# Softmax by pairs of tiles, the V halo sent ahead of the LN2 transposes, and h added to b2 by an accumulating DMA

## The chip, the cores and the metric

The kernel runs on one core of one Trainium2 chip. The metric is the time of one execution on the device, in microseconds (us). A profile comes from one of these executions. Its span is about 1.8 us shorter than the time that the device reports, so spans are compared with spans and times with times. Unless said otherwise, every execution named here was fast: within 1.5% of the fastest run of its kernel.

TensorE is called PE below, VectorE DVE, ScalarE ACT. SP is the engine that issues most DMAs, and POOL is GpSimd. The kernel has PE's sums written into PSUM, in pairs of banks named A to D, and uses a pair again once another engine has read it.

## The reference

One transformer layer on x of shape (1, 2048, 576), in bf16:

```python
h  = x + attention(layernorm(x)) @ wo      # 32 heads of 18, each position sees itself and 7 earlier ones, 2 apart
h2 = h + gelu(layernorm(h) @ w1 + b1) @ w2 + b2     # 4608 hidden units
```

The softmax of a position runs over 8 logits for each head.

## The kernel before

The 2048 positions are 16 tiles of 128, worked off as eight groups of two tiles. For each group PE does three things in a row: the first MLP matmul (L209, output `pm`), the output projection of the tiles of the *next* group (`pw`), and the second MLP matmul (`po`). The attention of the group after the next, and the second layernorm (LN2) of the next group, are meant to hide under these on DVE, ACT, POOL and the DMA engines.

This is how one group's normalized input `hnT` comes about, and PE's next group starts with it (shortened; `rstd` is one over the standard deviation of a row):

```python
def ln2_act(j):                 # statistics on ACT, rstd on POOL
    nc.scalar.activation(out=y, in_=h, func=Identity, scale=-1/D, accum_out=nmean)
    nc.scalar.activation(out=y, in_=h, func=Square, bias=nmean, accum_out=var)
    nc.scalar.activation(out=var, in_=var, func=Identity, scale=(1+EPS)/D, bias=eps2)
    nc.gpsimd.tensor_tensor(out=rstd, in0=var, in1=mhalf, op=ALU.pow)

def ln2_send(j):                # normalized rows to DRAM
    nc.scalar.activation(out=nmean, in_=nmean, func=Identity, scale=rstd)
    ln_apply_act(y, h, rstd, nmean)
    hn[j] = dma_out(y)          # two stores into td

def ln2_in(j):                  # and back, transposed
    nc.sync.dma_start_transpose(out=hnT_slot(j), in_=hn.pop(j))

def add_b2(j):                  # x of a tile becomes h + b2, the residual of the output
    nc.vector.tensor_tensor(out=x_all[:, j, :], in0=h_of.pop(j), in1=b2_bc, op=ALU.add)
```

The keys and values of 8 tiles lie in a ring. When tile j is done with the keys (or values), a DMA, the halo, replaces its slot by the same rows shifted by one, which the following tile of the same parity needs:

```python
def halo(j, t):                 # t = 1: keys, t = 2: values
    if j >= 2:
        ring = (None, k_ring, v_ring)[t]
        nc.sync.dma_start(out=ring[j % 2][:, j // 2, :], in_=kv_dram[j, 0:P, t - 1, :])
```

With c, d the tiles of the next group and e, f those of the one after, a middle group runs as follows (paraphrased; a visit is one of the parts into which the first matmul is cut; `m1[v]`: before visit v; `ia`, `ib`: before matmul row n of the second one, for its first and second tile):

```python
m1[0]: finish_out(previous), pv_t(d)                 # sums over V of the group's second tile
m1[3]: att_qk(e), w2_sums
ia[0]: exps(e), wo_visit(c, d), ln2_pair(c, d), att_den(e)
ia[2]: pv_sum(e), dma_tr_o(e)
ib[0]: finish_out(first)                             # output add: frees PSUM pair D
ib[2]: att_qk(f)
ib[32]: exps(f)
```

Of the kernel before, what the change touches and what calls it, by code (L numbers as in the profile page):

```python
# [17 lines left out]
def kernel(  # L18
# [13 lines left out]
    P = 128  # L32
# [49 lines left out]
    prod = wpool.tile([P, W, D], BF16, name="prod")  # L82

# [55 lines left out]
    def ln_stats(srcs, tag, c1, c0, bufs, first=None):  # L139
        n = len(srcs)  # L140
        stats = sb.tile([P, n, 2, nc.vector.BN_STATS_DIM], F32, tag=f"{tag}_stats", name=f"{tag}_stats", bufs=bufs)
        mv = sb.tile([P, n, nc.vector.BN_AGGR_DIM], F32, tag=f"{tag}_mv", name=f"{tag}_mv", bufs=bufs)
# [39 lines left out]

    def dma_out(src):
        td = dram.tile([P, KT * P], BF16, tag="td", name="td", bufs=4)
        nc.sync.dma_start(out=td[:, 0:D], in_=src)
        nc.sync.dma_start(out=td[:, D:KT * P], in_=src[:, KF * P:D])
        return td
# [121 lines left out]
    e_of = {}  # L309
# [16 lines left out]
    def att_qk_b(j, skip=0):  # L326
        att_qk_add(j, ((0, 0, 9), (0, 0, 4), (0, 0, 2), (0, 0, 1))[skip:])
        logits = sb.tile([P, W, H], F32, tag="logits", name="logits", bufs=2)
        nc.vector.tensor_tensor(out=logits[:], in0=prod[:, :, 0:H], in1=prod[:, :, 8 * H:9 * H], op=ALU.add)
        if j // 2 + 1 < W:  # L330
            nc.vector.memset(logits[0:1, j // 2 + 1:W, :], -1e9)
        mx = sb.tile([P, H], F32, tag="mx", name="mx")
        nc.vector.tensor_reduce(out=mx[:], in_=logits[:].rearrange("p w h -> p h w"), axis=AX.X, op=ALU.max)
        nc.vector.tensor_tensor(out=logits[:], in0=logits[:], in1=mx[:].unsqueeze(1).to_broadcast([P, W, H]),  # L334
                                op=ALU.subtract)
        e_of[j] = logits

    def att_qk(j):
        att_qk_a(j)
        halo(j, 1)  # L340
        att_qk_b(j)

    def att_exp(j):
        logits = e_of[j]
        nc.scalar.activation(out=logits[:], in_=logits[:], func=ACT.Exp, scale=SCALE)  # L345
# [5 lines left out]
    def att_den(j):  # L351
        e = e_of.pop(j)
        den = sb.tile([P, H], F32, tag="den", name="den")
        nc.vector.tensor_reduce(out=den[:], in_=e[:].rearrange("p w h -> p h w"), axis=AX.X, op=ALU.add)
        nc.vector.reciprocal(out=den[:], in_=den[:])
        a = sb.tile([P, W, H], BF16, tag="a", name="a")
        nc.vector.tensor_tensor(out=a[:], in0=e[:], in1=den[:].unsqueeze(1).to_broadcast([P, W, H]), op=ALU.mult)
        e_of[j] = a

    def att_pv_sum(j):  # L360
        a = e_of.pop(j)
        nc.vector.tensor_tensor(out=prod[:].rearrange("p w (d h) -> p w d h", h=H),  # L362
                                in0=v_ring[j % 2].rearrange("p w (d h) -> p w d h", h=H),
                                in1=a[:].unsqueeze(2).to_broadcast([P, W, Dh, H]), op=ALU.mult)
# [70 lines left out]
    def add_b2(j):  # L435
        nc.vector.tensor_tensor(out=x_all[:, j, :], in0=h_of.pop(j)[:], in1=b2_bc[:], op=ALU.add)

# [202 lines left out]
    with tc.manual_schedule(engines={ENG.PE, ENG.Activation, ENG.DVE, ENG.SP, ENG.Pool}):  # L640
# [83 lines left out]
        def ln2_pair(c, d, e, b2=True):  # L724
# [3 lines left out]
            for j in (c, d):  # L728
                if b2:
                    add_b2(j)  # L730
                ln2_send(j)
            for j in (c, d):
                ln2_in(j)
            if e is not None:
                att_den(e)

        loads = {v: [c_(load_w1, c)] for c, v in enumerate((3, 4, 9, 14, 16, 18))}
        for n, v in enumerate((20, 21, 22, 23)):
# [9 lines left out]
            7: [c_(att_qk_b, A[0]), c_(ln1_bias, 10), c_(ln1_act, 8, 3), c_(in_x, 0), c_(out_x, 1)],  # L748
            8: [c_(att_qk_a, A[1]), c_(att_qk_b, A[1]), c_(ln1_act, 9, 0)],
# [11 lines left out]
            20: [c_(ln2_rstd, A[1]), c_(add_b2, A[1]), c_(ln2_bias, A[1]), c_(att_qk_b, A[2], 1)],  # L761
# [57 lines left out]
        def exps(j):  # L819
            att_exp(j)  # L820
            gelu_table()
# [7 lines left out]
        for k, g in enumerate(GROUPS):  # L829
# [6 lines left out]
            if k == 0:  # L836
                m1[0] += [c_(halos, 1), c_(att_qk_a, d), c_(att_qk_b, d), c_(halo, d, 1)]
# [61 lines left out]
```

## Time and profile before

Time: 371.6 us (371.4 to 372.2, four runs), span 369.8 us.

From the page of the kernel before, the busy time of each engine with its share of the span and its number of instructions, and the shares of the chain of work that ended last:

```profile
PE 363.2 (98%) x4944; PEld 299.4 (81%) x4944; DVE 299.3 (81%) x452; ACT 239.1 (65%) x519; POOL 25.2 (7%) x35
...
PE 84%; DVE 11%; ACT 2%; POOL 1%; issue 1%; POOLq 0%; DVEq 0%
```

From the waits of PE in the kernel before (who waited for whom: us in total, times, longest):

```profile
PE busy L661 <- DVE prod L654: 1.5, 1, 1.5
PE pm L209 <- ACT hT L490: 0.5, 1, 0.5
PE o_pt L176 <- DVE h L407: 0.3, 1, 0.3
...
```

From its chain in order of time (start, length, what), one whole period of 37.7 us:

```profile
221.95 17.79 PE pm L209 x324
239.74 2.21 PE pw L209 x36
241.95 17.75 PE po L505 x144
259.70 17.79 PE pm L209 x324
```

PE is 98% busy, and from 79 to 366 us the chain is PE matmul but for a few pieces of 0.04 us or less. PE waits for nobody there. Whatever the other engines save cannot shorten this kernel; what they do too late can lengthen it. The slack is how long before PE starts on a group its `hnT` has landed.

PE's timeline, where it starts on it:

```profile
297.37 0.61 PE L209 MATMUL pm<-hnT,w_sb 64*128 64x256 bf16 x8
```

The second transpose is issued at 291.8 and lands 2.8 us later, at 294.6. PE starts at 297.4. The slack is 2.8 us. It is not the same in each group: worked out the same way it is 0.2 us for the second group, 2.8 for the fourth, 1.9 for the fifth, 2.4 for the sixth, and 0.8 for the eighth. For the third, the trace has lost a landing.

### The profile page before, as it was taken

What the parts mean: (1) busy time and instruction counts of PE and PEld (TensorE: products, weight loads), DVE (VectorE), ACT (ScalarE), POOL (GpSimd) and SP (SyncE); (2) the same over time, 40 slices, a digit from 0 to 9 for tenths busy, and PEclk for the clock granted to TensorE, in tenths of its full rate; (3) what the DMA queues carried; (4) which work ended last, traced back from release to release, by engine and by line L of the source; (5) the groups of instructions that cost most, each with busy time, mean ns of one, the idle gap of its engine ahead of it and who ended that gap; (6) DMA issues with size and microseconds to landing.
All of it is one profiled execution on the core that took longest, in us unless ns stands there. A gap on an engine that the chain in (4) does not pass through costs nothing.

```text
span 369.8 us, 11478 instructions
## 1 busy us (share of the span) xinstructions
PE 363.2 (98%) x4944; PEld 299.4 (81%) x4944; DVE 299.3 (81%) x452; ACT 239.1 (65%) x519; POOL 25.2 (7%) x35
## 2 busy tenths in 40 slices
PE   7999999999999999999999999999999999999996
PEld 4789877888788877887788778877887788778874
DVE  6899999999999798979897989889898986532332
ACT  2688756797738793679366936693669456735630
POOL 2322004000300010001000100000000000000000
PEclk9999999999999999999999999999999999999999
DMA  8979798956445104710431043104320411030000
GB/s 242 318 198 282 190 204 235 331 178 76 141 107 166 35 15 111 275 35 2 110 97 37 2 106 102 37 2 105 86 52 3 105 52 39 0 89 18 4 0 32
DMA packets 57265, 38.96 MB, mean 105 GB/s; under 512 B 31344, under 2 KB 55536, under 8 KB 57216
## 3 DMA queue, kind: packets, MB, share of 16 engines
q1 hardware_dynamic: 57056, 38.18, 38.6%
q8 instruction: 38, 0.62, 0.7%
q10 hardware_dynamic: 160, 0.07, 0.1%
q14 instruction: 11, 0.09, 0.1%
HBM read 19.92 MB, written 12.42 MB: 87 GB/s over the span
## 4 chain that ended last, share of the span: by engine, by line
PE 84%; DVE 11%; ACT 2%; POOL 1%; issue 1%; POOLq 0%; DVEq 0%
PE pm L209 37%; PE po L505 29%; PE po L576 8%; PE pw L209 5%; PE pq L209 4%; DVE ln_stats L145 2%; DVE prod L323 2%; DVE prod L362 1%; DVE prod L317 1%; PE busy L661 1%; DVE prod L366 1%; POOL ln_rstd L156 1%; ACT hT L490 1%; DVE ln_mv L146 1%; ACT L463 0%
## 5 line engine op out<-in xcount | busy, mean ns | idle before, releaser
L209 PE MATMUL pm<-hnT,w_sb 64*128 64x256 bf16 x2304 | 143.0, 269 | 0.5 <-ACT hT L490 0.5
L490 ACT ACTIVATE hT<-pm,b_sb 128x256 bf16<-128x256 f32 (+1 forms) x288 | 108.5, 498 | 48.4 <-PE pm L209 48.4
L209 PEld LDWEIGHTS <-w_sb 64*128 64x128 bf16 x2304 | 112.5, 94 | 15.0 <-issue 2.3
L505 PEld LDWEIGHTS <-hT 128*128 128x128 bf16 x864 | 84.0, 98 | 22.6 <-issue 1.7
L505 PE MATMUL po<-w2a_sb,hT 128*128 128x288 bf16 x672 | 84.5, 286 | 0.0
L209 PE MATMUL pq<-wq_sb,xnT 64*128 64x288 bf16 x768 | 54.0, 283 | 0.4 <-ACT xnT L255 0.2
L209 PEld LDWEIGHTS <-xnT 64*128 64x128 bf16 x864 | 44.1, 94 | 9.1 <-issue 0.4
L323 DVE TENSOR_TENSOR prod<-prod 128x2304 bf16<-128x2304 bf16 (+1 forms) x64 | 44.2, 691 | 2.1
L362 DVE TENSOR_TENSOR prod<-kv_ring,a 128x4608 bf16<-128x4608 bf16 x16 | 40.9, 2558 | 0.6
L317 DVE TENSOR_TENSOR prod<-kv_ring,q_all 128x4608 bf16<-128x4608 bf16 x16 | 40.8, 2552 | 0.2
L209 PE MATMUL pm<-hnT,w1h_sb 64*128 64x256 bf16 x288 | 39.4, 269 | 0.0
L366 DVE TENSOR_TENSOR prod<-prod 128x2304 bf16<-128x2304 bf16 (+1 forms) x32 | 33.9, 1058 | 1.1
L345 ACT ACTIVATE logits<-logits 128x256 f32<-128x256 f32 x16 | 6.7, 417 | 38.1 <-DVE logits L334 38.1
L423 POOL TENSOR_TENSOR ln_rstd<-ln_var,mhalf 128x1 f32<-128x1 f32 x14 | 11.3, 810 | 249.8 <-ACT ln_var L422 249.6
L505 PE MATMUL po<-w2b_sb,hT 128*128 128x288 bf16 x192 | 25.5, 286 | 0.0
L294 ACT CAST kv_ring<-pq 128x576 bf16<-128x576 f32 x32 | 19.4, 641 | 8.4 <-PE pq L209 8.4
L407 DVE TENSOR_TENSOR h<-pw,x_all 128x576 f32<-128x576 f32 x16 | 11.4, 751 | 14.0 <-PE pw L209 14.0
L209 PE MATMUL pw<-wo_sb,oT 64*128 64x288 bf16 x256 | 19.5, 283 | 0.2
L463 ACT ACT_TABLE_LOAD x14 | 18.0, 1283 | 0.2
L552 DVE TENSOR_TENSOR prod<-hT 128x512 f16<-128x512 f16 (+1 forms) x8 | 3.6, 455 | 17.6 <-ACT hT L490 17.6
L209 PEld LDWEIGHTS <-oT 64*128 64x128 bf16 x288 | 13.9, 94 | 4.3 <-POOLq L219 0.8
L345 ACT ACT_TABLE_LOAD x13 | 16.7, 1283 | 0.2
(98 smaller groups left out, 340.4 us busy)
## 6 DMA issues: line engine op xcount, KB each, us to landing
w_sb<-in_B_w_dram SPq DMA_DIRECT2D x6, 768.0 KB, 6.0
kv_ring<-kv_dram SPq DMA_DIRECT2D x28, 144.0 KB, 2.8
w2a_sb<-in_B_w_dram SPq DMA_DIRECT2D x4, 1008.0 KB, 6.5
kv_dram<-kv_ring SPq DMA_DIRECT2D x13, 288.0 KB, 3.5
out_dram<-o_sb SPq DMA_DIRECT2D x15, 144.0 KB, 2.9
td<-q_all SPq DMA_DIRECT2D x14, 144.0 KB, 2.4
td<-hn SPq DMA_DIRECT2D x14, 144.0 KB, 1.8
wq_sb<-in_A_wqkv_dram SPq DMA_DIRECT2D x3, 576.0 KB, 5.9
```

The costliest lines, as they stand in the source:

```text
L209: last = nc.tensor.matmul(duo["g"][r ^ swap][i], lhsT=lhsT, rhs=rhs, start=(swap == 0 and i == 0 and kt == 0), stop=(swap == 1 and kt == K ...
L294: pace[0] = nc.scalar.copy(out=dst.rearrange("p (d g h) -> p g d h", g=2, h=H // 2), in_=ps[:, :, 0:HALF].rearrange("p g (h d) -> p g d h" ...
L317: nc.vector.tensor_tensor(out=prod[:], in0=k_ring[j % 2], in1=q_all[:, j, :].unsqueeze(1) .to_broadcast([P, W, D]), op=ALU.mult)
L323: nc.vector.tensor_tensor(out=prod[:, :, o * H:o * H + n], in0=prod[:, :, a * H:a * H + n], in1=prod[:, :, c * H:c * H + n], op=ALU.add)
L345: nc.scalar.activation(out=logits[:], in_=logits[:], func=ACT.Exp, scale=SCALE)
L362: nc.vector.tensor_tensor(out=prod[:].rearrange("p w (d h) -> p w d h", h=H), in0=v_ring[j % 2].rearrange("p w (d h) -> p w d h", h=H), in ...
L366: nc.vector.tensor_tensor(out=prod[:, 0:n, :], in0=prod[:, 0:n, :], in1=prod[:, n:2 * n, :], op=ALU.add)
L407: nc.vector.tensor_tensor(out=h[:].rearrange("p (g c) -> p g c", g=2), in0=pw[:, :, 0:HALF], in1=x_all[:, j, :].rearrange("p (g c) -> p g ...
L463: nc.scalar.activation(out=warm[:], in_=mhalf[:], func=ACT.Gelu_apprx_tanh)
L490: pace[0] = nc.scalar.activation(out=hT[us[i // GF]][:, GF * r + i % GF, 0:N], in_=ps[:, r, i * N:(i + 1) * N], func=ACT.Gelu_apprx_tanh, ...
L505: nc.tensor.matmul(banks[half], lhsT=hT[f // (2 * GF)][:, f % (2 * GF), i * P:(i + 1) * P], rhs=w2_rows(f)[:, half * HALF:(half + 1) * HAL ...
L576: nc.tensor.matmul(bank, lhsT=l, rhs=r, start=(start and m == 0), stop=(m == NM - 1), skip_group_check=True)
```

## The change

The intent is to relieve DVE and ACT. From the second group on the two tiles e, f of a pair share one maximum, exponential, denominator and division (on 512 columns instead of twice 256). The 14 late additions of b2 leave DVE: SP copies b2 into x, and an accumulating DMA from GpSimd adds h, after the stores of LN2. The V halo of e is issued ahead of the LN2 transposes, so that f's sum over V, which now follows soon after e's, finds it. The core of the diff, with cuts:

```diff
+    def put_b2(j):
+        nc.sync.dma_start(out=x_all[:, j, :], in_=b2_bc[:])
+
+    def accumulate_h(j):
+        ins = nc.gpsimd.dma_start(out=x_all[:, j, :], in_=h_of.pop(j)[:], accum_op=ALU.add).ins
+        tc.add_manual_dep(ins, sent[0].name, sync_dep, reason="behind the transfers of LN2")
 ...
-        def ln2_pair(c, d, e, b2=True):
+        def ln2_pair(c, d, js=()):
             for j in (c, d):
                 ln2_h(j)
                 ln2_act(j)
             for j in (c, d):
-                if b2:
-                    add_b2(j)
+                put_b2(j)
+            if js:
+                att_den(*js)
+                att_pv_sum(js[0])
+            for j in (c, d):
                 ln2_send(j)
             for j in (c, d):
+                accumulate_h(j)
+            if js:
+                halo(js[0], 2)
+            for j in (c, d):
                 ln2_in(j)
-            if e is not None:
-                att_den(e)
+            if js:
+                dma_tr_o(js[0])
 ...
-                    m1[3] = m1.get(3, []) + [c_(att_qk, e)] + [c_(w2_sums, *m) for m in T_SUMS.get(k, ())]
-                    ia[0] = [c_(exps, e)]
-                ia[0] = ia.get(0, []) + [c_(wo_visit, (c, "B"), (d, "C")), c_(ln2_pair, c, d, e)]
 ...
+                elif e is not None:
+                    m1[1] = [c_(att_qk_pair, e, f)]
+                    m1[3] = [c_(w2_sums, *m) for m in T_SUMS.get(k, ())]
+                    ia[0] = [c_(exps, e, f), wo, c_(ln2_pair, c, d, (e, f))]
 ...
-                    ia[2] = [c_(pv_sum, e), c_(dma_tr_o, e)]
-                    ib[2] = [c_(att_qk, f)] + ([c_(halos, 7)] if k == 1 else [])
-                    ib[32] = [c_(exps, f)]
+                    ib[2] = [c_(pv_sum, f), c_(dma_tr_o, f)]
```

`att_qk_pair(e, f)` does the key products of e, issues e's K halo, finishes e's logits, and goes straight on to f, which needs that halo. The second group has an order of its own: there the exponential of the pair comes after LN2.

More of the change, by code (lines that the diff above doesn't have):

```diff
@@ L82 @@
     prod = wpool.tile([P, W, D], BF16, name="prod")
+    logits = wpool.tile([P, 2, W, H], F32, name="logits")
+    probs = wpool.tile([P, 2, W, H], BF16, name="probs")
+    peak = wpool.tile([P, 2, H], F32, name="peak")
+    den = wpool.tile([P, 2, H], F32, name="den")
     qp_cm = tc.tile_pool(name="qkvw", bufs=1)
@@ L140, in ln_stats @@
         n = len(srcs)
-        stats = sb.tile([P, n, 2, nc.vector.BN_STATS_DIM], F32, tag=f"{tag}_stats", name=f"{tag}_stats", bufs=bufs)
-        mv = sb.tile([P, n, nc.vector.BN_AGGR_DIM], F32, tag=f"{tag}_mv", name=f"{tag}_mv", bufs=bufs)
+        pool = qp if tag.startswith("ln1") else sb
+        stats = pool.tile([P, n, 2, nc.vector.BN_STATS_DIM], F32, tag=f"{tag}_stats", name=f"{tag}_stats", bufs=bufs)
+        mv = pool.tile([P, n, nc.vector.BN_AGGR_DIM], F32, tag=f"{tag}_mv", name=f"{tag}_mv", bufs=bufs)
         for i, src in enumerate(srcs):
@@ L180, in transpose_in @@
         nc.tensor.transpose(pt[0:HP, KF, :], src[:, KF * P:D], ident[:])
+    sent = [None]
     def dma_out(src):
@@ L185, in dma_out @@
         nc.sync.dma_start(out=td[:, 0:D], in_=src)
-        nc.sync.dma_start(out=td[:, D:KT * P], in_=src[:, KF * P:D])
+        sent[0] = nc.sync.dma_start(out=td[:, D:KT * P], in_=src[:, KF * P:D]).ins
         return td
@@ L306, in tr_b1, with sides @@
         nc.scalar.copy(out=b1_sb[:], in_=pt)
-    e_of = {}
+    side = {}
+    def sides(js):
+        i = side[js[0]]
+        return slice(i, i + len(js))
     def halo(j, t):
@@ L324, in att_qk_add, with att_qk_b, att_max, att_qk_rest @@
                                     in1=prod[:, :, c * H:c * H + n], op=ALU.add)
-    def att_qk_b(j, skip=0):
+    def att_qk_b(j, i, skip=0):
+        side[j] = i
         att_qk_add(j, ((0, 0, 9), (0, 0, 4), (0, 0, 2), (0, 0, 1))[skip:])
-        logits = sb.tile([P, W, H], F32, tag="logits", name="logits", bufs=2)
-        nc.vector.tensor_tensor(out=logits[:], in0=prod[:, :, 0:H], in1=prod[:, :, 8 * H:9 * H], op=ALU.add)
+        nc.vector.tensor_tensor(out=logits[:, i], in0=prod[:, :, 0:H], in1=prod[:, :, 8 * H:9 * H], op=ALU.add)
         if j // 2 + 1 < W:
-            nc.vector.memset(logits[0:1, j // 2 + 1:W, :], -1e9)
-        mx = sb.tile([P, H], F32, tag="mx", name="mx")
-        nc.vector.tensor_reduce(out=mx[:], in_=logits[:].rearrange("p w h -> p h w"), axis=AX.X, op=ALU.max)
-        nc.vector.tensor_tensor(out=logits[:], in0=logits[:], in1=mx[:].unsqueeze(1).to_broadcast([P, W, H]),
-                                op=ALU.subtract)
-        e_of[j] = logits
-    def att_qk(j):
+            nc.vector.memset(logits[0:1, i, j // 2 + 1:W, :], -1e9)
+    def att_max(js):
+        n, sl = len(js), sides(js)
+        nc.vector.tensor_reduce(out=peak[:, sl], in_=logits[:, sl].rearrange("p i w h -> p i h w"), axis=AX.X, op=ALU.max)
+        nc.vector.tensor_tensor(out=logits[:, sl], in0=logits[:, sl],
+                                in1=peak[:, sl].unsqueeze(2).to_broadcast([P, n, W, H]), op=ALU.subtract)
+    def att_qk_rest(j, i, skip=0):
+        att_qk_b(j, i, skip)
+        att_max([j])
+    def att_qk(j, i):
         att_qk_a(j)
         halo(j, 1)
-        att_qk_b(j)
-    def att_exp(j):
-        logits = e_of[j]
-        nc.scalar.activation(out=logits[:], in_=logits[:], func=ACT.Exp, scale=SCALE)
+        att_qk_rest(j, i)
+    def att_qk_pair(e, f):
+        for i, j in enumerate((e, f)):
+            att_qk_a(j)
+            halo(j, 1)
+            att_qk_b(j, i)
+        att_max([e, f])
+    def att_exp(*js):
+        sl = sides(js)
+        nc.scalar.activation(out=logits[:, sl], in_=logits[:, sl], func=ACT.Exp, scale=SCALE)
     def att_pv(j):
@@ L349, in att_pv, with att_den @@
         att_pv_sum(j)
-    def att_den(j):
-        e = e_of.pop(j)
-        den = sb.tile([P, H], F32, tag="den", name="den")
-        nc.vector.tensor_reduce(out=den[:], in_=e[:].rearrange("p w h -> p h w"), axis=AX.X, op=ALU.add)
-        nc.vector.reciprocal(out=den[:], in_=den[:])
-        a = sb.tile([P, W, H], BF16, tag="a", name="a")
-        nc.vector.tensor_tensor(out=a[:], in0=e[:], in1=den[:].unsqueeze(1).to_broadcast([P, W, H]), op=ALU.mult)
-        e_of[j] = a
+    def att_den(*js):
+        n, sl = len(js), sides(js)
+        nc.vector.tensor_reduce(out=den[:, sl], in_=logits[:, sl].rearrange("p i w h -> p i h w"), axis=AX.X, op=ALU.add)
+        nc.vector.reciprocal(out=den[:, sl], in_=den[:, sl])
+        nc.vector.tensor_tensor(out=probs[:, sl], in0=logits[:, sl],
+                                in1=den[:, sl].unsqueeze(2).to_broadcast([P, n, W, H]), op=ALU.mult)
     def att_pv_sum(j):
-        a = e_of.pop(j)
+        a = probs[:, side.pop(j)]
         nc.vector.tensor_tensor(out=prod[:].rearrange("p w (d h) -> p w d h", h=H),
                                 in0=v_ring[j % 2].rearrange("p w (d h) -> p w d h", h=H),
-                                in1=a[:].unsqueeze(2).to_broadcast([P, W, Dh, H]), op=ALU.mult)
+                                in1=a.unsqueeze(2).to_broadcast([P, W, Dh, H]), op=ALU.mult)
         for n in (4, 2):
@@ L747 @@
             6: [c_(ln1_rstd, 10), c_(ln1_act, 8, 2), c_(halo, A[0], 1)],
-            7: [c_(att_qk_b, A[0]), c_(ln1_bias, 10), c_(ln1_act, 8, 3), c_(in_x, 0), c_(out_x, 1)],
-            8: [c_(att_qk_a, A[1]), c_(att_qk_b, A[1]), c_(ln1_act, 9, 0)],
+            7: [c_(att_qk_rest, A[0], 0), c_(ln1_bias, 10), c_(ln1_act, 8, 3), c_(in_x, 0), c_(out_x, 1)],
+            8: [c_(att_qk_a, A[1]), c_(att_qk_rest, A[1], 1), c_(ln1_act, 9, 0)],
             9: [c_(halo, A[1], 1), c_(in_x, 1)],
@@ L760 @@
             19: [c_(ln2, A[1])],
-            20: [c_(ln2_rstd, A[1]), c_(add_b2, A[1]), c_(ln2_bias, A[1]), c_(att_qk_b, A[2], 1)],
+            20: [c_(ln2_rstd, A[1]), c_(add_b2, A[1]), c_(ln2_bias, A[1]), c_(att_qk_rest, A[2], 0, 1)],
         }
@@ L817, in halos, with exps @@
                 store_halo(pending_halo.pop(0))
-        def exps(j):
-            att_exp(j)
+        def exps(*js):
+            att_exp(*js)
             gelu_table()
@@ L836 @@
             if k == 0:
-                m1[0] += [c_(halos, 1), c_(att_qk_a, d), c_(att_qk_b, d), c_(halo, d, 1)]
+                m1[0] += [c_(halos, 1), c_(att_qk_a, d), c_(att_qk_rest, d, 1), c_(halo, d, 1)]
                 mid[0] = [c_(exps, d)]
-                m1[1] = [c_(pv_t, c), c_(pv_t, d), c_(load_w2, 4), c_(att_qk, e)]
+                m1[1] = [c_(pv_t, c), c_(pv_t, d), c_(load_w2, 4), c_(att_qk, e, 0)]
                 ia[0] = [c_(wo_visit, (c, "B"))]
-                ia[12] = [c_(exps, e), c_(wo_visit, (d, "A")), c_(ln2_pair, c, d, e, False), c_(pv_sum, e), c_(dma_tr_o, e), c_(halos, 2)]
+                ia[12] = [c_(exps, e), c_(wo_visit, (d, "A")), c_(ln2_pair, c, d, (e,)), c_(halos, 2)]
@@ L842 @@
                 ib[0] = [c_(finish_out, g[0])]
-                ib[4] = [c_(att_qk, f)]
+                ib[4] = [c_(att_qk, f, 1)]
                 ib[32] = [c_(exps, f)]
             elif c is not None:
-                m1[0].append(c_(pv_t, d))
+                wo = c_(wo_visit, (c, "B"), (d, "C"))
                 if k == 1:
-                    m1[0] += [c_(add_b2, j) for j in g]
-                if e is not None:
-                    m1[3] = m1.get(3, []) + [c_(att_qk, e)] + [c_(w2_sums, *m) for m in T_SUMS.get(k, ())]
-                    ia[0] = [c_(exps, e)]
@@ L852 @@
-                ia[0] = ia.get(0, []) + [c_(wo_visit, (c, "B"), (d, "C")), c_(ln2_pair, c, d, e)]
+                    m1[0].append(c_(pv_t, d))
+                    m1[1] = [c_(att_qk_a, e), c_(halo, e, 1), c_(att_qk_b, e, 0), c_(halos, 7)]
+                    m1[3] = [c_(att_qk_a, f), c_(halo, f, 1)]
+                    ia[0] = [wo, c_(ln2_pair, c, d), c_(att_qk_b, f, 1), c_(att_max, (e, f)), c_(exps, e, f), c_(att_den, e, f)]
+                    ia[2] = [c_(pv_sum, e), c_(dma_tr_o, e)]
+                elif e is not None:
+                    m1[1] = [c_(att_qk_pair, e, f)]
+                    m1[3] = [c_(w2_sums, *m) for m in T_SUMS.get(k, ())]
+                    ia[0] = [c_(exps, e, f), wo, c_(ln2_pair, c, d, (e, f))]
+                else:
+                    ia[0] = [wo, c_(ln2_pair, c, d)]
```

## The prediction

> **What bounds the kernel.** TensorE. The page gives PE 98% busy. In the chain of waits everything from 79 to 366 us is PE matmul without a gap. PE's waits for other engines add to 2.7 us, 1.5 us of it before the first matmul; none is listed after 73 us. A period of one group is 37.7 us (17.8 first MLP matmul, 2.2 output projection, 17.7 second), run five times, then two shorter ones. DVE (81%) and ACT (65%) matter only where they make PE wait.
>
> **What the change removes.** The 14 late b2 adds: 0.75 us each, 10.5 us of DVE. In the five pairs from the second group on, ten softmaxes become five: from the 256- and 576-column f32 operations (425 and 751 ns) an operation costs about 0.16 us beside its columns, so five merged operations save about 0.8 us a pair, 4 us in all. On ACT one exponential with its two table loads and the dummy GELU (1.28+1.28+0.20+0.16 us) goes per pair: about 14 us. Expect DVE busy near 285 us, ACT near 225 us.
>
> **What it adds.** Per group two SP copies of b2 into x, and two accumulating DMAs from GpSimd. The Trainium skill ("DMA: Bandwidth & Descriptors", "SWDGE vs HWDGE vs iDMA") says that accumulation and casting must be issued from GpSimd, and that all issuers share the same 16 DMA engines; the trace of before has no such DMA, so their length is unknown. They wait for the LN2 stores, so they run while the LN2 transposes do.
>
> **What lies on the critical path.** Nothing of the savings: PE has no wait that they could end. The deadlines are what count:
> 1. LN2 transposes. In the timeline of the fourth group they are issued by SP at 215.7 and 217.0 us and land 2.9 us later, about 220.0; PE starts on them at 221.9. Slack 1.9 us. For the last group it is about 0.8 us (issued 328.0 and 329.3, needed at 333.0). The doubled exponential delays ACT by about 0.27 us, the V halo costs SP 0.5 us that it spends waiting anyway, and the accumulates compete for DMA engines: I guess 0.3 to 1 us. So the slack is mostly eaten; a PE wait of 0 to 0.5 us is possible, likeliest in the last group.
> 2. In the second group the pair is late on DVE: exponential near 137 us, sums over V end near 150.5, so the output add that frees PSUM pair C ends near 151.3; PE wants C near 151.5. Wait 0 to 0.5 us.
> 3. Later groups: the second sum over V waits for the halo (lands about 3 us after 215.2), ends near 223; the add that frees C ends near 224, wanted at 227. Fits.
> 4. GpSimd carries the markers between matmul halves. Both accumulates should be issued by 219, the next marker is due at 223. Fits.
>
> **Predicted time.** 371.8 us, range 370.0 to 374.5. Faster by over 2%: 0.01; within 2%: 0.92; slower by over 2%: 0.07.
>
> **What would show each step.** PE still 98%, chain still bare matmul, DVE down about 14 us and ACT about 14 us: right. A PE wait for the DMA of hnT at the start of a group's first MLP matmul: point 1 was too kind. PE waiting for the output add at the start of the third group: point 2. PE waiting for GpSimd's queue: point 4. Start-up to 108 us should be unchanged within 0.5 us.
>
> **What would make it wrong.** Accumulating DMAs that take 4 us or more each and hold up the transposes: 1 to 2 us a group, 7 to 14 us in all. Or GpSimd held up while generating descriptors.

## More of the kernel before

`h` is a tile with two buffers. The last two groups use a faster scheme for the second matmul, whose two remainder buffers `rest` and `part` share the buffers of `h`:

```python
rest, part = (sb.tile([P, D], F32, tag="h", name="rest", bufs=2) for _ in range(2))
```

The start of the seventh group (group 6, counted from 0) serves as the example. First, SP's timeline of the kernel before (start, length on the queue, instruction, output<-input): two stores for each tile, the second tile's at 289.50, and then both transposes.

```profile
289.50 0.33 SPq L185 DMA_DIRECT2D td<-hn  x1
289.89 0.42 SPq L186 DMA_DIRECT2D td<-hn  x1
290.48 2.52 SPq L433 DMA_TRANSPOSE hnT<-td  x2
293.10 0.53 SPq L314 DMA_DIRECT2D kv_ring<-kv_dram  x1
```

The instructions on tile hnT in that window (duration, first and last start; then the time from issue to landing):

```profile
L433 SPq DMA_TRANSPOSE hnT<-td x2: 1204/1216/1227, 290.5 to 291.8; - x2
...
DMA to landing us min/median/max: 2.8/2.8/2.8
```

## The result, and the profile after

The changed kernel takes 376.2 us (374.3, 376.7, 375.7, 377.5) against 371.6 us. The ratio of the fast runs is 1.012 (95% interval 1.009 to 1.015). Here and below a ratio is the mean time of one kernel's fast runs over that of the other's in the same rounds, so it is not quite the ratio of the medians quoted. The change is 1.2% slower: within the 2% band, but outside the range predicted (370.0 to 374.5). It also scatters over 3 us where the kernel before keeps within 0.8.

The profile of the changed kernel fell on the fastest of these runs (374.27 us, span 372.5). From its page, the busy times, the chain, and the two large DMA queues (packets, MB, share of 16 engines' span):

```profile
PE 362.7 (97%) x4944; PEld 303.0 (81%) x4944; DVE 285.8 (77%) x413; ACT 225.0 (60%) x499; POOL 43.2 (12%) x49
...
q1 hardware_dynamic: 59072, 40.24, 40.3%
q0 software_dynamic: 2016, 2.07, 5.1%
...
PE 55%; DVE 28%; DMA 5%; ACT 4%; issue 3%; POOL 2%; SPq 2%; POOLq 0%; DVEq 0%; ACTq 0%
```

The savings came in full: DVE 299.3 to 285.8 us, ACT 239.1 to 225.0. But the chain is no longer bare matmul; 45% of it is now something else (16% before, nearly all of that ahead of 79 us), most of it DVE. The waits of PE in that profile:

```profile
PE pm L216 <- DVE rest L627: 1.2, 1, 1.2
...
PE pm L216 <- DVE logits L342: 0.6, 1, 0.6
...
PE pm L216 <- DMA hnT<-td: 0.3, 1, 0.3
```

(L216 is the line of the matmul that was L209.) The wait put down to `logits L342` is at the start of the second group, where the last transpose landed at 109.12 us, 0.14 us before PE began. Nothing in that matmul reads `logits`, so this too is a wait for `hnT`, put down to something that happened to end at the time.

**Second look, the same kernel.**

> The changed kernel unedited, for its spread and a second trace. Expected as in the first four runs: median near 376 us, runs from 374 to 378, while the kernel before keeps within 0.3 us of 371.6. Both theories expect the PE waits at the start of a group's first MLP matmul (hnT arriving late) and at the start of the last group; a slower execution should show more or longer ones of these.

It took 376.3 us (376.0 to 376.7, four runs), ratio 1.012 (1.011 to 1.013). Its profile (span 374.4 us) has the waits of PE:

```profile
PE pm L216 <- DMA hnT<-td: 2.6, 3, 1.3
PE busy L689 <- DVE prod L682: 1.5, 1, 1.5
PE pm L216 <- DVE rest L627: 1.0, 1, 1.0
```

By group the waits at the start of the first MLP matmul are 1.3 us (second group), 0.35 (fourth), 0.9 (seventh), and 1.0 for the remainder buffers (eighth), together 3.6 of the 4.6 us by which the span grew. Another 0.5 us had arisen before the second group, in the loading phase, which differs by up to 0.9 us between the traces and has nothing to do with the change; the rest is spread in pieces below 0.35 us.

The same group as before, the seventh, in this second profile. SP's timeline:

```profile
293.68 0.33 SPq L192 DMA_DIRECT2D td<-hn  x1
294.06 0.43 SPq L193 DMA_DIRECT2D td<-hn  x1
294.59 0.40 SPq L325 DMA_DIRECT2D kv_ring<-kv_dram  x1
295.16 2.54 SPq L454 DMA_TRANSPOSE hnT<-td  x2
```

The instructions on tile hnT in this window:

```profile
L454 SPq DMA_TRANSPOSE hnT<-td x2: 1212/1217/1222, 295.2 to 296.5; - x2
...
DMA to landing us min/median/max: 2.8/3.5/4.1
```

PE's timeline, with the wait in brackets:

```profile
300.61 0.61 PE L216 MATMUL pm<-hnT,w_sb 64*128 64x256 bf16 x8 [0.94 <-DMA hnT<-td]
```

And POOL's timeline: the two rstd of LN2, and then the accumulates.

```profile
288.69 0.56 POOL L444 TENSOR_TENSOR ln_rstd<-ln_var,mhalf 128x1 f32<-128x1 f32 x1 [29.61 <-ACT ln_var L443]
290.58 1.85 POOL L444 TENSOR_TENSOR ln_rstd<-ln_var,mhalf 128x1 f32<-128x1 f32 x1 [1.33 <-ACT ln_var L443]
296.21 1.78 POOL L463 DMA_DIRECT2D x_all<-h  x2 [3.79 <-DMA td<-hn]
```

The first transpose still lands in 2.8 us. The second, beside which the two accumulates run, takes 4.1. But that is only part of it. ACT's timeline in both profiles shows where LN2 starts; of the kernel before:

```profile
281.59 0.42 ACT L345 ACTIVATE logits<-logits 128x256 f32<-128x256 f32 x1
...
283.43 0.67 ACT L420 ACTIVATE hn<-h 128x576 bf16<-128x576 f32 x1
```

and of the changed kernel:

```profile
283.82 0.63 ACT L368 ACTIVATE logits<-logits 128x512 f32<-128x512 f32 x1
...
286.53 0.68 ACT L441 ACTIVATE hn<-h 128x576 bf16<-128x576 f32 x1 [0.56 <-DVE h L428]
...
292.46 0.29 ACT L449 ACTIVATE ln_nmean<-ln_nmean,ln_rstd 128x1 f32<-128x1 f32 x1 [0.94 <-POOL ln_rstd L444]
```

Counting every event back from the moment PE was free for the group (297.37 us before; 300.61 - 0.94 = 299.67 us after), the slack of 2.8 us was spent like this:

| Step | before | after | later by |
|---|---|---|---|
| LN2 begins on ACT, before PE is free | 13.94 | 13.14 | 0.80 (0.21 longer exponential, 0.56 waiting for h) |
| from there to the second tile's store | 6.07 | 7.15 | 1.08 (0.94 of it waiting for rstd) |
| from the store to the second transpose | 2.3 | 2.8 | 0.5 (the V halo stands between) |
| second transpose, issue to landing | 2.8 | 4.1 | 1.3 |
| sum | | | 3.7 |

2.8 - 3.7 = -0.9: PE waits 0.94 us. No single item is larger than the slack. This is the group with the largest sum, and the wait for h is in this group of this profile alone; the first profile has none. In the fourth group, where PE waits in both profiles (0.29 and 0.35 us), the same four steps are 0.15, 1.3, 0.55 and 1.05 us, again a little more than its slack of 2.8.

Why is h late, and rstd slow? The waits of DVE in this second profile have two lines that the kernel before does not have at all: waits for halos, 22 us in total.

```profile
DVE prod L328 <- DMA kv_ring<-kv_dram: 14.6, 5, 4.5
DVE prod L383 <- DMA kv_ring<-kv_dram: 7.7, 5, 2.9
```

L328 is the key product: f's, right behind e's, waits for e's K halo (2.9 us on average, up to 4.5). L383 is the product with V, of f behind e. Alternating the tiles had hidden these transfers; pairing them puts their latency into DVE's line. Pairing is not all of it: `dve_add` below, which has the pairs and no accumulates, has 5.7 and 6.5 us in these two lines. Why they are longer with the accumulates, no run separates. DVE's 13.5 us of saved work is more than spent again on waiting. And DVE now multiplies with V just when POOL computes rstd:

```profile
289.46 2.56 DVE L383 TENSOR_TENSOR prod<-kv_ring,probs 128x4608 bf16<-128x4608 bf16 x1
```

The second rstd begins at 290.58 inside this instruction and ends at 292.43, 0.4 us after it. The Trainium skill ("SBUF — State Buffer", "Who interferes with whom") says that a DVE instruction with two SBUF inputs contends with a GpSimd instruction that reads SBUF, and that the second one to come is blocked until the first is done. This trace agrees: 0.56 us for the rstd that ended before the product began, 1.85 us for the one that fell into it. In the kernel before, POOL's timeline of the same group is

```profile
285.56 0.92 POOL L423 TENSOR_TENSOR ln_rstd<-ln_var,mhalf 128x1 f32<-128x1 f32 x1 [35.30 <-ACT ln_var L422]
287.45 0.55 POOL L423 TENSOR_TENSOR ln_rstd<-ln_var,mhalf 128x1 f32<-128x1 f32 x1 [0.97 <-ACT ln_var L422]
```

There the product with V ended at 286.08, so it met the first rstd only, which ended at 286.48, again 0.4 us after it; and nothing waited for that one.

### The profile page after: what moved, and what is told of

Read it like the earlier page. It is cut to its first block, busy times and chain, and to the rows that moved or that the text cites. A ratio compares the mean times of both kernels' runs of the same rounds, so it can differ in the third digit from the quotient of the medians.

```text
span 372.5 us, 11484 instructions
## 1 busy us (share of the span) xinstructions
PE 362.7 (97%) x4944; PEld 303.0 (81%) x4944; DVE 285.8 (77%) x413; ACT 225.0 (60%) x499; POOL 43.2 (12%) x49
## 3 DMA queue, kind: packets, MB, share of 16 engines
q1 hardware_dynamic: 59072, 40.24, 40.3%
## 4 chain that ended last, share of the span: by engine, by line
PE 55%; DVE 28%; DMA 5%; ACT 4%; issue 3%; POOL 2%; SPq 2%; POOLq 0%; DVEq 0%; ACTq 0%
PE pm L216 30%; PE po L533 14%; DVE prod L334 5%; PE po L604 5%; DVE prod L383 4%; DVE prod L328 4%; DVE prod L387 3%; PE pw L216 3%; DVE ln_stats L150 2%; DMA hnT<-td 2%; PE pq L216 2%; ACT hT L518 1%; POOL ln_rstd L161 1%; DVE peak L346 1%; DMA x_all<-h 1%
## 5 line engine op out<-in xcount | busy, mean ns | idle before, releaser
L216 PE MATMUL pm<-hnT,w_sb 64*128 64x256 bf16 x2304 | 143.0, 269 | 2.7 <-DVE rest L627 1.2
L216 PEld LDWEIGHTS <-w_sb 64*128 64x128 bf16 x2304 | 116.1, 94 | 14.1 <-issue 3.5
L216 PE MATMUL pq<-wq_sb,xnT 64*128 64x288 bf16 x768 | 54.1, 283 | 0.3 <-ACT kv_ring L301 0.2
L216 PEld LDWEIGHTS <-xnT 64*128 64x128 bf16 x864 | 44.0, 94 | 9.1 <-issue 0.4
L328 DVE TENSOR_TENSOR prod<-kv_ring,q_all 128x4608 bf16<-128x4608 bf16 x16 | 40.9, 2553 | 13.7 <-DMA kv_ring<-kv_dram 13.6
L383 DVE TENSOR_TENSOR prod<-kv_ring,probs 128x4608 bf16<-128x4608 bf16 x16 | 40.9, 2557 | 7.8 <-DMA kv_ring<-kv_dram 7.4
L444 POOL TENSOR_TENSOR ln_rstd<-ln_var,mhalf 128x1 f32<-128x1 f32 x14 | 16.6, 1186 | 211.5 <-ACT ln_var L443 211.5
L216 PE MATMUL pm<-hnT,w1h_sb 64*128 64x256 bf16 x288 | 39.9, 269 | 0.0
L216 PE MATMUL pw<-wo_sb,oT 64*128 64x288 bf16 x256 | 19.5, 283 | 0.2
L161 POOL TENSOR_TENSOR ln_rstd<-ln_veps,mhalf 128x1 f32<-128x1 f32 (+2 forms) x13 | 13.2, 1018 | 48.9 <-DVE ln_veps L155 42.6
L216 PEld LDWEIGHTS <-oT 64*128 64x128 bf16 x288 | 14.1, 94 | 4.0 <-POOLq L226 0.8
L463 POOL DMA_DIRECT2D x_all<-h x14 | 12.7, 1057 | 27.6 <-DMA td<-hn 19.4
L216 PEld LDWEIGHTS <-w1h_sb 64*128 64x128 bf16 x288 | 14.7, 94 | 1.2
```

The source lines that it names most:

```text
L161: nc.gpsimd.tensor_tensor(out=rstd[:], in0=veps[:], in1=mhalf[:].to_broadcast([P, n]), op=ALU.pow)
L216: last = nc.tensor.matmul(duo["g"][r ^ swap][i], lhsT=lhsT, rhs=rhs, start=(swap == 0 and i == 0 and kt == 0), stop=(swap == 1 and kt == K ...
L328: nc.vector.tensor_tensor(out=prod[:], in0=k_ring[j % 2], in1=q_all[:, j, :].unsqueeze(1) .to_broadcast([P, W, D]), op=ALU.mult)
L383: nc.vector.tensor_tensor(out=prod[:].rearrange("p w (d h) -> p w d h", h=H), in0=v_ring[j % 2].rearrange("p w (d h) -> p w d h", h=H), in ...
L444: nc.gpsimd.tensor_tensor(out=rstd[:], in0=var[:], in1=mhalf[:], op=ALU.pow)
L463: ins = nc.gpsimd.dma_start(out=x_all[:, j, :], in_=h_of.pop(j)[:], accum_op=ALU.add).ins
```

## The experiments

Two theories stood at the start. A: the accumulating DMAs are the cost, since they share the DMA engines with the transposes and hold `h`. B: the new order is the cost, since it makes LN2 late. All medians below are beside the kernel before in the same rounds (371.4 to 371.8).

### b2 added by DVE instead of the accumulates

```diff
-            for j in (c, d):
-                put_b2(j)
 ...
-                accumulate_h(j)
+                add_b2(j)
```

> Changed kernel, but b2 is added to h by DVE at the place in program order where the accumulating DMA was; no copies of b2, no accumulates. Theory A (the accumulates compete with the LN2 transposes for DMA engines, and keep h busy at the end of the seventh group): the transposes land in 2.9 us again, no wait for the remainder add, time 371.5 to 372.3 and a spread of under 0.5 us. Theory B (LN2 itself is late: the sums over V now run on DVE while GpSimd computes rstd, the exponential is doubled, the V halo comes first): little gained, 374 to 377.

Measured: 372.2 us (371.4 to 372.5), ratio 1.0005 (0.9993 to 1.0018). No wait of PE beyond those of the kernel before. All its transposes of hnT:

```profile
L454 SPq DMA_TRANSPOSE hnT<-td x14: 1199/1208/1222, 104.3 to 328.4; - x14
...
DMA to landing us min/median/max: 2.8/2.9/3.8
```

The second transpose mostly lands in 2.8 to 3.1 us (once 3.8), and the slack in the fourth to seventh groups is 0.9 to 1.4 us, where the kernel before has 1.9 to 2.8. So without the copies and accumulates nothing is lost (its runs scatter over 1.1 us, where under 0.5 was expected). But LN2 is as late as theory B says: the rstd of these groups take 1.3 to 2.3 us, 1 us or more of the slack is gone, and what is left happens to be enough.

### The accumulates alone, in the kernel before

The copies and accumulates replace `add_b2` in the kernel before; pairs and halo stay as they were.

```diff
             for j in (c, d):
-                if b2:
-                    add_b2(j)
+                put_b2(j)
+            for j in (c, d):
                 ln2_send(j)
+            for j in (c, d):
+                accumulate_h(j)
             for j in (c, d):
                 ln2_in(j)
 ...
```

> Kernel before, with only the b2 copies and the accumulating DMAs behind the LN2 transfers; softmaxes single and the V halo behind the transposes as before. Theory A: most of the loss is there, 373.5 to 376, with spread. Theory B: 371.5 to 373 (only the 1.2 us wait of the remainder add in the seventh group).

Measured: 373.3 us (373.1 to 374.0), ratio 1.0043 (1.0029 to 1.0057). The waits of PE:

```profile
PE pm L211 <- DVE rest L608: 1.2, 1, 1.2
```

The second transpose takes 4.0 to 4.9 us from the third group on, but only the fifth group waits for it, 0.08 us; in the third, fourth, sixth and seventh 1.3 us of slack or more stay. The loss is the remainder buffers. So theory A alone explains 1.6 us, theory B alone nothing, and both together 4.5. The two do not add, because both draw on the same slack, and only what is beyond it reaches PE.

### The remainder buffers out of h

```diff
-        rest, part = (sb.tile([P, D], F32, tag="h", name="rest", bufs=2) for _ in range(2))
+        rest, part = (wo_sb[:].rearrange("p k d -> p (k d)").bitcast(F32)[:, n * D:(n + 1) * D] for n in range(2))
```

(wo is no longer needed when they are written, and is just as large.)

> Changed kernel, but the two remainder buffers of the last two groups lie in the memory of wo instead of sharing the buffers of h, so they do not wait for the accumulates to have read h. Both theories: the 1.2 us PE wait for the remainder add at the start of the last group goes; time 0.5 to 1.3 us below the changed kernel (0.5 if the transposes of the last group land at that time too). If nothing is gained, that wait was the transposes' own.

Measured: 374.9 us (374.0 to 375.4), ratio 1.0079: 1.3 us under the changed kernel. The wait for `rest` is gone; the waits for `hnT` are still there (1.25, 0.45, 0.4 and 0.4 us; the first is again put down to an uninvolved instruction). An accumulate that reads h keeps its buffer until it has landed, 4 us after it was issued, where `add_b2` had released it in 0.75 us.

### The accumulates moved away

With the remainder buffers as above, the accumulates go to the third visit of the next group's first matmul (and no longer depend on the LN2 stores).

```diff
-            for j in (c, d):
-                accumulate_h(j)
 ...
+            if k > 0:
+                m1[2] = [c_(accumulate_h, j) for j in g] + m1.get(2, [])
```

> Changed kernel, with the remainder buffers in the memory of wo (as own_rest) and the accumulating DMAs moved into the third visit of the next group's first MLP matmul, far from the LN2 transposes. Same DMAs, same bytes. Theory A (the accumulates hurt only because they run beside the second LN2 transpose): that transpose lands in 2.9 us again, no PE wait on hnT, 371.6 to 372.6. A rival (accumulates hurt wherever they are, by GpSimd's queue, which also carries the markers between matmul halves): 374 or more, with PE waits on GpSimd's queue.

Measured: 373.1 us in the fast runs (372.8 to 374.0), ratio 1.0041 (1.0027 to 1.0056). The profiled run was slow (422 us, granted clock 0.85) and is not used. The kernel was therefore run again:

> The same kernel as accum_late, whose profile fell in a slow execution (granted clock 0.85), for a profile of a fast one; fast executions of accum_late took 372.8 to 374.0, 1.5 us over the kernel before. Expected: 373.2 again; the second transpose lands in 2.9 us and the slack before hnT is 1 to 1.5 us as in dve_add. Where its last 1.5 us go is open: a rival says at GpSimd's queue (waits of PE on it in the third visit), theory A says at the second group's hnT alone.

Measured: 372.6 us (372.3 to 373.7), ratio 1.0034. The second transpose is back at 2.9 to 3.1 us, no wait on POOL's queue is listed, and the waits at the group starts have shrunk to 0.1 us. So the place of the accumulates is what counts, not their existence. But the slack expected did not come back: it is 0.2 and 0.7 us in the fourth and sixth groups, and the fifth and seventh have none, for there PE still waits 0.1 us. The reason is in DVE's waits: 16.5 us for K halos, more than before the move. In their new place the accumulates meet the K halo that DVE waits for (one issued at 267.3 us, beside accumulates issued at 266.8 and 267.4, takes 5.4 us to land), and h comes later still: ACT waits for it three times, 2.3 us in all.

### The accumulates moved ahead of LN2

The opposite move, with `h` shared as in the changed kernel: copies and accumulates before the statistics.

```diff
             for j in (c, d):
                 ln2_h(j)
+                put_b2(j)
+            for j in (c, d):
+                accumulate_h(j)
+            for j in (c, d):
                 ln2_act(j)
 ...
```

> Changed kernel, with the b2 copies and accumulates ahead of LN2's statistics in program order instead of behind the LN2 stores; the buffers of h stay shared. DMA engines have nothing else then. Theory A: the second transpose lands in 2.9 us, no remainder wait; the accumulates hold GpSimd for 1.8 us just before rstd, so LN2 may be up to 1 us later, which the slack of 0.9 to 1.4 us of dve_add barely covers: 371.7 to 373.5. If it stays at 376, where the accumulates stand does not matter.

Measured: 377.1 us (375.6 to 379.7), ratio 1.016 (1.011 to 1.020): a miss. The transposes are quick again (median 3.0 us) and the remainder wait is gone, as expected. But in POOL's program the rstd of LN2 now stand behind accumulates that wait for the copies of b2. In the second group these are issued at 100.5 us and rstd is done at 103.7 us instead of the 101.6 of the kernel before, the store goes out 2.7 us later, and PE waits 2.3 us, until `hnT` has landed. The profile fell on the slowest of its runs. It proves no more than that this place is worse: a late LN2 costs as much as slow transposes.

### The V halo behind the transposes again

```diff
-            if js:
-                halo(js[0], 2)
             for j in (c, d):
                 ln2_in(j)
+            if js:
+                halo(js[0], 2)
```

> Changed kernel, with the V halo back behind the LN2 transposes, the only edit. Decomposing the lost slack gave 0.55 us to the halo: from the issue of the second LN2 store to that of the second transpose 2.79 us where the kernel before has 2.24. Expected: 2.24 us again, PE waits on hnT shorter by about 0.5 us each, so 375.3 to 375.8 against 376.2 (the groups that wait do so by 0.3 to 1.3 us), unless the second sum over V, which then gets its halo later, makes PE wait instead; then no gain.

Measured: 384.0 us (382.3 to 384.8), ratio 1.032: a miss, neither a gain nor "no gain". From the second store to the second transpose it is 2.3 us again, so the half microsecond on SP is real, and the waits for `hnT` did shorten (0.7 us in total). But PE now waits for something else:

```profile
PE pm L216 <- DVE o_sb L660: 7.1, 4, 2.3
```

Behind the transposes the halo also meets the accumulates. In the fourth group it is issued at 223.0 us and DVE gets it at 227.4. f's sum over V, and behind it the output add that frees a PSUM pair (`o_sb`), come so late that PE waits up to 2.3 us for the pair. So moving the halo ahead is needed by the pairing, and is not the fault.

### The exponential behind LN2 in every group

```diff
-                    ia[0] = [c_(exps, e, f), wo, c_(ln2_pair, c, d, (e, f))]
+                    ia[0] = [wo, c_(ln2_pair, c, d), c_(exps, e, f), c_(att_den, e, f)]
+                    ia[2] = [c_(pv_sum, e), c_(dma_tr_o, e)]
```

The remainder buffers are out of h here too.

> Changed kernel, with the remainder buffers in the memory of wo, and with the exponential of the pair behind LN2 in ACT's order in every group, as the second group has it (its hnT landed 4.7 us early while all others were late). Accumulates stay beside the transposes. If the loss is one of slack, as the decomposition says: waits on hnT of the fourth to seventh groups vanish, only that of the second group (0.6 to 1.3 us) stays: 372.5 to 373.3 against 374.9 for own_rest. If the accumulates slow PE in another way than through hnT: unchanged near 374.9.

Measured: 385.7 us (385.0 to 387.5), ratio 1.038. Half of the expectation held: the waits for `hnT` of the fourth to seventh groups are gone, though the accumulates are still beside the transposes (second transpose 4.0 to 4.2 us), and only the second group's 1.1 us is left. (The slack is 1.7 us in the fourth group, before which nothing disturbs PE; in the later ones PE itself is late, which flatters it.) The other half failed, for the same reason as with the halo:

```profile
PE pm L216 <- DVE o_sb L660: 8.0, 4, 3.2
```

DVE stands idle for the exponential (7.4 us in the fourth group) and the output add is late. This run also gives the test of rstd. With DVE idle beside it, POOL's timeline in the fourth group reads

```profile
214.25 0.56 POOL L444 TENSOR_TENSOR ln_rstd<-ln_var,mhalf 128x1 f32<-128x1 f32 x1 [32.89 <-ACT ln_var L443]
216.14 0.55 POOL L444 TENSOR_TENSOR ln_rstd<-ln_var,mhalf 128x1 f32<-128x1 f32 x1 [1.33 <-ACT ln_var L443]
```

and all eight rstd of the fourth to seventh groups take 0.55 or 0.56 us, where the changed kernel has 0.56 to 2.6.

Not all that these last three runs lose is waiting. The clock record of their profiles has stretches of 3.41 us at half the TensorE clock: one with the accumulates ahead of LN2 (from 112.4 us), one with the halo behind (193.5), two here (193.6 and 275.6). No other profile of a fast run has one inside the run of groups. Each began within 1.5 us of the end of a PE wait of 2.2 us or more; one such wait (2.3 us, with the halo behind) was not followed by one, and none followed the waits of 1.7 us or less. Half speed for 3.41 us costs about 1.7 us, an estimate that one group confirms: the second group of the run with the accumulates ahead took 39.4 us instead of 37.7, though PE waited for nothing inside it.

### A plain casting copy instead of the accumulate

```diff
-in_=h_of.pop(j)[:], accum_op=ALU.add).ins
+in_=h_of.pop(j)[:]).ins
```

> Changed kernel, with the accumulate turned into a plain casting copy of h over x at the same place and queue (wrong on purpose: b2 is lost). The page of the changed kernel gives the 14 accumulates 5.1% of the 16 engines' span, 1.36 us of all 16 each. If reading the destination and adding is what makes them dear: their share halves, the second transpose takes near 3.3 us instead of 3.9, time 374.5 to 375.5. If casting or the queue itself is dear: same share, same time as the changed kernel, 376.

Measured: 375.9 us (375.1 to 376.6). Its output is wrong, which doesn't matter for the time. The queue's share went from 5.1% to 4.1%, the waits of PE for `hnT` are 3.2 us in total, and the second transpose takes 3.8 to 4.7 us. The share neither halved nor stayed: the adding is a fifth of it. But it is not the adding that disturbs the transposes. A casting transfer of the same size on the same queue disturbs them as much. Whether that is the cast, the queue or the 288 KB of f32 that it reads was not separated. Per DMA, 4.1% of 374.8 us over 14 is 1.1 us of all sixteen engines for the copy, and 5.1% of 372.5 us over 14 is 1.36 us for the accumulate.

### The copies of b2 alone

DVE adds h to the b2 that SP has copied into x.

```diff
-                accumulate_h(j)
+                nc.vector.tensor_tensor(out=x_all[:, j, :], in0=h_of.pop(j)[:], in1=x_all[:, j, :], op=ALU.add)
```

> Changed kernel, with the b2 copies by SP kept, and h added to them by DVE where the accumulate was issued. Tells the copies from the accumulates. Expected: the copies land before the LN2 stores begin, so they cost nothing: 372 to 372.5 as dve_add. If the copies were part of the loss: 373 or more.

Measured: 373.4 us in the fast runs (373.3 to 373.9; one slow run of 379.8), ratio 1.0055. The experiment was badly built. In the second group nothing stands between the copy and the addition, so DVE must wait for the copy; its whole line is late there, and the output add holds PE for 1.5 us. This one wait is more than the difference from `dve_add`'s 372.2, which was measured in other rounds. Whether the copies cost anything themselves is left open; against the kernel before, 1.9 us less this wait leaves 0.4 us.

### The known conflicts taken away

The remainder buffers out of h; the accumulates in the fourth visit, meant to be clear of transposes and K halo; and the sums over w2 between the two key products of a pair, so that the K halo travels under them.

```diff
-                    m1[1] = [c_(att_qk_pair, e, f)]
-                    m1[3] = [c_(w2_sums, *m) for m in T_SUMS.get(k, ())]
+                    m1[1] = [c_(att_qk_a, e), c_(halo, e, 1), c_(att_qk_b, e, 0)]
+                    m1[1] += [c_(w2_sums, *m) for m in T_SUMS.get(k, ())]
+                    m1[1] += [c_(att_qk_a, f), c_(halo, f, 1), c_(att_qk_b, f, 1), c_(att_max, (e, f))]
 ...
```

> Changed kernel with all the conflicts taken away: remainder buffers in the memory of wo; the accumulates issued in the fourth visit of the next group's first MLP matmul, clear of the transposes and of the K halo; and the sums over w2 placed between the two QK products of a pair, so that the K halo travels under them. The theory (the change hurts through DMA latencies that now stand in DVE's line, and through accumulates beside transfers that something waits for) expects: DVE's waits for halos fall from 21 us to under 9 us, the wait of ACT for h goes, the slack before hnT is 1 us or more in the third to sixth groups, time 371.5 to 372.4, the same as the kernel before, since PE has nothing to gain. If it stays at 372.6 to 373.2 (accum_late) or above, something else holds PE.

Measured: 372.7 us (372.1 to 373.6), ratio 1.0029 (1.0015 to 1.0042): above the range expected, and where the expectation says that something else holds PE. The slack before `hnT` is 1.25 to 1.5 us in the fourth to seventh groups, as expected. DVE's waits for K halos fell:

```profile
DVE prod L383 <- DMA kv_ring<-kv_dram: 11.6, 4, 3.0
DVE prod L328 <- DMA kv_ring<-kv_dram: 4.2, 2, 3.2
```

but those for V halos rose, so together they are 15.8 us, not under 9; ACT still waits for h once, 0.9 us. The one wait of PE left that the kernel before does not have is in the third group, on the output add:

```profile
PE pm L216 <- DVE o_sb L659: 0.8, 1, 0.8
```

This is the late pair of the second group. The second group has an order of its own, and there the accumulates in their new place meet the K halo. POOL, SP and DVE in that group:

```profile
120.32 1.97 POOL L463 DMA_DIRECT2D x_all<-h  x2 [18.05 <-PE pm L216]
121.82 0.94 SPq L325 DMA_DIRECT2D kv_ring<-kv_dram  x1
127.71 2.56 DVE L328 TENSOR_TENSOR prod<-kv_ring,q_all 128x4608 bf16<-128x4608 bf16 x1 [3.15 <-DMA kv_ring<-kv_dram]
```

The halo takes 5.9 us to land, and DVE waits 3.15 us for it; in `dve_add` the same halo takes 3.3 us and DVE waits 0.42. So one conflict was left, and no run removes it. Even so most of the loss of 4.5 us has been taken away by removing conflicts alone, with all the added DMAs still there. The new place of the sums over w2 bought slack and no time: `accum_late2`, without it, took 372.6 us. None of the versions is faster than the kernel before, and none could be expected to be: PE has the same 363 us of matmul in all of them.

## Why the prediction was wrong, point by point

**What bounds the kernel, and what the change removes: right.** DVE was predicted near 285 us and measured 285.8, ACT near 225 and measured 225.0; none of it shortened anything. "Nothing of the savings" lies on the critical path: right. The predicted step "PE still 98%, chain still bare matmul" fell with the next point. So did "start-up to 108 us should be unchanged within 0.5 us": PE began the second group 0.6 and 1.8 us later in the two profiles, because it waited there for `hnT`.

**Point 1, the LN2 transposes: the step that failed.** The prediction named the right place and then put the terms of its sum too low. "So the slack is mostly eaten; a PE wait of 0 to 0.5 us is possible, likeliest in the last group." PE waited for `hnT` 1.0 us in all in the first profile and 2.6 us in the second, in the second, fourth and seventh groups. In the last group `hnT` came in time, and PE waited for the remainder buffers. In the trace:

- The slack was read at two places only, from the timeline of the fourth group (which prepares the fifth) and for the last, and put at 1.9 and 0.8 us. The second group has 0.2 us and was not looked at. Its wait was the longest one on `hnT` in both profiles (0.6 and 1.3 us), although LN2 is not late there: the halo on SP (0.2 to 0.3 us) and the slower second transpose (0.4 and 1.3 us) were enough.
- "The doubled exponential delays ACT by about 0.27 us": 0.21 us, right.
- "The V halo costs SP 0.5 us that it spends waiting anyway": it costs 0.5 us that nothing hid, and the second transpose is issued that much later.
- "The accumulates compete for DMA engines: I guess 0.3 to 1 us": 1.0 to 1.3 us on the second transpose in most groups.
- Two terms were missing altogether, 1.5 us in the example: rstd on POOL, blocked by the product with V that the new order puts beside it (0.9), and h, late because DVE waits for halos (0.6, in this group of the second profile alone).

With these the sum is 3.7 us in the seventh group, against a slack of 2.8; the prediction's own terms give 0.6 to 1.3.

**A step that the prediction did not have: the life of h.** The accumulates hold the buffers of h, and the remainder buffers share them. 1.0 to 1.2 us, shown by the run with separate buffers.

**Point 2, the pair of the second group:** right. In both profiles of the changed kernel the add ends 4.9 us after PE's start on the third group. In the last experiment PE asked for the pair 5.2 us after that start, so the margin is 0.3 us. There, with the K halo slowed by the accumulates, the add came 0.8 us too late.

**Point 3, later groups: "Fits."** It fits, and the times were close (the add that frees C ends 2.4 us after PE's start in the fifth group, 2.1 predicted). But the two experiments that moved something there cost 8 us (the halo, against the changed kernel) and 11 us (the exponential, against the version with its own remainder buffers), of which about 1.7 and 3.4 us are the stretches at half clock: there is little room.

**Point 4, POOL and its markers:** right; no wait of PE on POOL's queue appeared. But the instruction of POOL that mattered was another one, rstd.

**What would make it wrong:** "accumulating DMAs that take 4 us or more each and hold up the transposes". They do take 4.0 us at the median from issue to landing, and they do hold up the transposes, by about 1 us a group; the 7 to 14 us written there was too much, because the slack pays the first part. The other danger named, GpSimd held up, did not come: it was busy 1.06 us on each accumulate, and no wait of PE for its queue is listed.

What stays open: how fast the last variant would be without its one conflict in the second group, the cost of the b2 copies if any, and why the loading phase differs by up to 0.9 us between traces. That a transpose lands later beside the accumulates is shown; that sharing the DMA engines is the reason is argued only. Also, the table above is of one group; in the others the terms are alike but not equal.

## What to carry to other kernels

Where PE is the bound and everything else hides beneath it, savings on other engines are worth nothing, and each change spends slack; so list the slack of *every* deadline in *every* group first, and add up what the change takes from it, since losses that fit singly do not fit together. Work saved by putting two dependent tiles back to back can be lost again, because the transfer between them was hidden only by the alternation. When an operation moves from a compute engine to a DMA, ask what it runs beside, and how much longer it holds its source.

## What the Trainium skill lacked or had wrong

- "DMA: Bandwidth & Descriptors" ("SWDGE vs HWDGE vs iDMA") says that accumulation and casting must be issued from GpSimd, and "Issuing engines are not separate DMA queues" that all issuers share the 16 engines; the first no run here tests, and with the second it agrees that POOL's transfers slow SP's transposes (2.8 to 4.1 us in the example). The page gives no cost of such a transfer. Here a 144 KB accumulate from f32 into bf16 took 1.36 us of all sixteen engines and 4.0 us from issue to landing at the median, a plain casting copy 1.1 and 3.7 us. An average 144 KB of the ordinary queue took 0.55 us (40.3% of 372.5 us for 40.24 MB). The page's fit for this path in "Anatomy of one DMA" (2.0 us plus bytes over 436 GB/s) would give 2.3 us, an estimate for 144 KB; the measurement decides.
- The same page ("Rules for kernel authors") says "A transpose next to ordinary DMAs needs nothing". That is about correct results. In time, a second transpose that lands in 2.8 to 3.2 us in the kernel before mostly took 3.8 to 5.1 us beside two such transfers. The page has no number for it.
- "SBUF — State Buffer" ("Who interferes with whom") was right about GpSimd being blocked by a DVE instruction with two SBUF inputs. What it does not give is how long a blocked GpSimd compute instruction looks in a profile: one on a single column, 0.55 us alone, showed as 1.85 us, and up to 2.8 us in these runs.
